# Unit 0's first loads, the clearing of padding and the table of steps in a kernel of gated linear attention followed by a rational feed-forward layer

## The chip, the cores and the metric

The kernel runs on one core of a Trainium2 chip. Its time is the device time of one execution in microseconds (us). The time before is the median of three runs; one further execution was taken with the hardware profiler, and its own time stands in the table below.

## What is computed

For each of 4 batches and 8 heads, with 768 time steps and 48 channels per head, a state of 48 x 48 is decayed and updated at each step, and read by q. The output of all heads, 3072 rows of 384, goes through two matrices with a rational function between them.

```python
f = 1.0 / (1.0 + np.exp(-f_logit))
for t in range(S):
    state = f[:, :, t, :, None] * state + np.einsum('bhd,bhe->bhde', k[:, :, t], v[:, :, t])
    y[:, :, t] = np.einsum('bhd,bhde->bhe', q[:, :, t], state)
...
h = x @ w_in                                   # 384 -> 2048
P = a[0] + a[1] * h + a[2] * h2 + a[3] * h3
Q = 1.0 + np.abs(b[0]) * np.abs(h) + np.abs(b[1]) * h2
out = (P / (Q + 1e-06)) @ w_out                # 2048 -> 384
```

## The kernel before

The work is cut into 12 units: 3 stretches of 256 time steps, each for the 4 batches in turn. Unit n + 4 continues the state of unit n. Within a unit, 256 steps are two chunks of 128 (index j), and the 8 heads are four pairs (index a).

Nothing is scheduled automatically. The string `ORDER` is a table of 815 steps, and the program is written out in that order. Each engine then works through its own instructions strictly in the order in which they stand, so the table alone sets what waits behind what. A step is a short name, the unit, and a range; `@0` to `@3` names one of four slots of PSUM, and a step that takes a slot waits until the slot's last reader is done.

The steps, with the engine that they run on, and the name of the tile by which the profile shows them:

- **Loads.** `ld n f`, `ld n k`, `ld n q` are issued on SP's DMA queue (L194), `ld n v` on POOL's, since it converts to bf16. `wi` and `wo` load the two weight matrices in pieces on POOL's queue (L201, four DMAs to a step, and L205). `ab_` loads the four numbers a and the two numbers b, copied to all 128 partitions, on SP (L209, L211).
- **Constants.** `ca`, `cb` build triangular masks and the identity on POOL. `cz` clears tiles on DVE with memsets (L232): `zeros`, `lsp`, `qkp`, `vmp` and the states. Of `lsp` and `qkp` each head has 64 columns, of which 48 are written later and 16 stay zero. `cc` builds a mask on DVE. `fa` and `fb` turn a and b into scaled coefficients `sig` on DVE, with one Ln on ACT (L264).
- **Attention, unit n.** `ef` and `ls`: Exp and Ln of the gates on ACT (L279 to fn, L284 to lsp). `cs`: sums over time on PE. `A n 0` and `A n 1`: Exp of these on ACT (L304, which needs `sig`, and L306). `xa n 0` and `xa n 1`: q and k times A, to qkp on DVE (L311). `T`, `Te`: transposes on PE (tp) and their copy on DVE (qkT, L330). `sc`, `mk`: scores on PE (L343) and their masking on DVE (scm, L351). `vm`: a shifted copy of v on POOL (vmp, L358). `ya`, `yb`: sv, the sums for the state, and y on PE; y needs qkT, scm and vmp. `ae`, `st`: the state's decay on ACT and the new state on DVE (L423). `ye`: y is copied to bf16 on ACT (xT, L414).
- **Feed-forward, unit n.** `h`: matmul with w_in on PE (hp, L432), 4 of 16 blocks to a step. `hy`: copy to bf16 on ACT (hy, L446). `sq` on DVE or `sa` on ACT: the square (h). `ab`: the absolute value on DVE (z, L458). The denominator z + h is summed on PE (`u`) and goes to `ln` on ACT (L474); or it is summed by `zd`, a DMA on POOL's queue that adds h into z (L483), or by `zv` on DVE, and goes to `lz` on ACT (lq, L490). `ex`: Exp on ACT (qi, L498). `p1`, `p2`, `pm`: the numerator's parts on DVE (gall and hy). `ta` adds them by a DMA on POOL's queue (L517), `tv` on DVE. `gm`: times qi on DVE (L526). `o`: matmul with w_out on PE (op, L533). `oe`: copy of the result (osb, L548), `so`: store on SP.

Unit 0 is loaded and worked on in two halves of the heads, `0 2` (the low ones) and `2 4` (the high ones).

Of the kernel before, what the change touches and what calls it, by code (L numbers as in the profile page):

```python
# [24 lines left out]
yb 0 2 4; st 0 1; yb 0 0 2; ld 2 q; ye 0; h 0 4 8 @2; ef 1; ld 2 f; ls 1; h 0 0 4 @3; hy 0 4 8
cs 1 @0; hy 0 0 4; h 0 8 12 @2; A 1 0; sq 0 0 8; A 1 1; p1 0 0 8; hy 0 8 12; h 0 12 16 @0; wo 4 8
xa 1 0; wo 12 16; ab 0 0 8; ld 2 k; wo 0 4; hy 0 12 16; xa 1 1; u 0 4 8 @2; wo 8 12; p2 0 0 8
T 1 @3; ln 0 4 8; p1 0 8 16; vm 1 0; ya 1 0 @0 @1; Te 1; ld 2 v; u 0 0 4 @2; ae 1; vm 1 1; ld 3 q
st 1 0; sc 1 0 @3; ln 0 0 4; ab 0 8 16; ya 1 1; mk 1 0; ld 3 f; ef 2; sc 1 1 @2; ex 0 0 8; mk 1 1
st 1 1; yb 1; sq 0 8 16; ls 2; ye 1; cs 2 @1; pm 0 0 8; u 0 12 16 @2; A 2 1; p2 0 8 16; u 0 8 12 @0  # L30
A 2 0; pm 0 8 16; ln 0 12 16; h 1 4 8 @3; ld 3 k; xa 2 0; ln 0 8 12; h 1 8 12 @2; tv 0 8 16
sa 1 4 8; h 1 12 16 @0; tv 0 0 8; hy 1 4 8; hy 1 8 12; xa 2 1; h 1 0 4 @1; hy 1 12 16; gm 0 0 8
T 2 @2; sa 1 0 4; ab 1 8 16; o 0 0 0 4 @0; sq 1 8 16; hy 1 0 4; o 0 0 4 8; ex 0 8 16; vm 2 0
o 0 1 0 4; Te 2; ld 3 v; u 1 8 12 @1; ab 1 0 8; vm 2 1; ld 4 q; u 1 12 16 @2; ln 1 8 12; p1 1 0 16
u 1 0 4 @3; ln 1 12 16; ld 4 f; gm 0 8 16; sc 2 1 @1; o 0 1 4 8; ef 3; pm 1 8 16; u 1 4 8 @2; ld 4 k
ln 1 0 4; o 0 1 8 12; mk 2 1; ls 3; o 0 0 8 12; ln 1 4 8; vm 3 1; o 0 0 12 16; p2 1 0 16; ld 4 v
cs 3 @1; ex 1 8 16; vm 3 0; o 0 1 12 16; ld 5 q; pm 1 0 8; ta 1 8 16; ya 2 0 @2 @3; ta 1 0 8; A 3 1
ld 5 f; ae 2; A 3 0; xa 3 1; ld 5 k; ef 4; st 2 0; sc 2 0 @1; xa 3 0; ya 2 1; oe 0 0 2 s; ls 4
mk 2 0; so 0 0 2; T 3 @0; ex 1 0 8; st 2 1; yb 2; Te 3; cs 4 @3; ld 6 q; vm 4 1; ye 2; ld 5 v
sc 3 0 @0; A 4 1; sc 3 1 @1; mk 3 0; vm 4 0; h 2 12 16 @2; A 4 0; mk 3 1; h 2 0 4 @3; hy 2 12 16  # L40
gm 1 8 16; ya 3 0 @1 @0; hy 2 0 4; xa 4 1; h 2 8 12 @2; sa 2 0 4; gm 1 0 8; ae 3; h 2 4 8 @3
hy 2 8 12; ld 6 f; st 3 0; xa 4 0; ef 5; ya 3 1; sa 2 4 8; ab 2 8 16; ld 6 k; T 4 @2; st 3 1; ls 5
sq 2 8 16; yb 3; hy 2 4 8; cs 5 @0; Te 4; ye 3; u 2 12 16 @3; ld 7 q; A 5 0; ab 2 0 8; h 3 12 16 @2
p1 2 0 16; ln 2 12 16; zd 2 0 8; sc 4 0 @1; ld 6 v; A 5 1; xa 5 0; h 3 0 4 @3; hy 3 12 16; vm 5 0
p2 2 0 16; ld 7 f; vm 5 1; u 2 8 12 @0; ef 6; hy 3 0 4; xa 5 1; h 3 4 8 @2; ld 7 k; pm 2 8 16
ln 2 8 12; o 1 0 0 4 @3; ld 8 q; hy 3 4 8; o 1 1 0 4; mk 4 0; ta 2 8 16; h 3 8 12 @0; ex 2 8 16
ab 3 0 8; pm 2 0 8; ya 4 0 @1 @2; hy 3 8 12; sq 3 0 8; ta 2 0 8; o 1 1 4 8; ls 6; sc 4 1 @0
ab 3 8 16; o 1 0 4 8; zd 3 0 8; ae 4; lz 2 0 8; mk 4 1; o 1 0 8 12; o 1 0 12 16; st 4 0; ld 8 f
cs 6 @0; ef 7; sq 3 8 16; ya 4 1; ex 2 0 8; p1 3 0 16; ld 8 k; yb 4; o 1 1 8 12; vm 6 0; st 4 1
ye 4; o 1 1 12 16; vm 6 1; pm 3 8 16; ld 7 v; u 3 8 12 @2; A 6 0; pm 3 0 8; oe 1 0 2 s; h 4 12 16 @1  # L50
ln 3 8 12; so 1 0 2; p2 3 0 16; u 3 12 16 @3; hy 4 12 16; h 4 8 12 @2; xa 6 0; ta 3 8 16; ln 3 12 16
gm 2 8 16; ld 9 q; h 4 0 4 @1; A 6 1; ta 3 0 8; hy 4 8 12; gm 2 0 8; T 5 @0; sa 4 0 4; xa 6 1
o 2 0 0 4 @2; hy 4 0 4; Te 5; o 2 0 4 8; lz 3 0 8; o 2 1 0 4; sq 4 8 16; sc 5 1 @0; o 2 1 4 8
ld 9 f; mk 5 1; o 2 1 8 12; ef 8; ya 5 0 @1 @3; ex 3 0 8; ld 9 k; ab 4 8 16; zv 4 8 16; sc 5 0 @0
# [12 lines left out]
hy 6 0 4; mk 7 1; o 4 1 8 12; ex 5 0 8; zv 6 8 16; o 4 1 12 16; ya 7 0 @3 @0; ab 6 0 8; sa 6 0 4
p1 6 0 16; o 4 0 4 8; ae 7; o 4 0 8 12; ls 9; zd 6 0 8; st 7 0; o 4 0 12 16; ex 5 8 16; p2 6 0 16
ya 7 1; yb 7; pm 6 8 16; oe 4 0 2 s; cs 8 @1; vm 9 0; ye 7; st 7 1; cs 9 @2; so 4 0 2; vm 9 1
pm 6 0 8; ld 10 v; A 8 1; h 7 4 8 @3; A 8 0; xa 8 1; ta 6 8 16; h 7 0 4 @0; ef 11; xa 8 0; ta 6 0 8  # L70
ld 11 k; hy 7 4 8; h 7 12 16 @1; gm 5 8 16; ld 11 q; hy 7 0 4; gm 5 0 8; A 9 0; T 8 @3; hy 7 12 16
h 7 8 12 @0; xa 9 0; A 9 1; Te 8; o 5 0 0 4 @1; lz 6 0 8; o 5 1 0 4; sq 7 0 8; sc 8 0 @3; sc 8 1 @2
mk 8 0; hy 7 8 12; o 5 1 4 8; o 5 1 8 12; ex 6 0 8; mk 8 1; o 5 0 4 8; ya 8 0 @3 @0; ab 7 8 16
lz 6 8 16; xa 9 1; o 5 0 8 12; p1 7 0 16; o 5 0 12 16; o 5 1 12 16; ae 8; ls 10; st 8 0; T 9 @2
# [40 lines left out]
def kernel(  # L115
# [113 lines left out]
    def zero(t):  # L229
        f = t.rearrange({2: "p a -> p a", 3: "p a b -> p (a b)", 4: "p a b c -> p (a b c)",  # L230
                         5: "p a b c d -> p (a b c d)"}[len(t.shape)])
        nc.vector.memset(f.bitcast(F32), 0.0)  # L232

    def const_z(i):
        if i == 0:
            zero(zeros)
            zero(lsp[0])
            nc.vector.memset(ind, 0.0)
# [349 lines left out]
```

## Time and profile before

| what | value |
| --- | --- |
| median of 3 runs | 240.35 us (240.1 to 240.41) |
| the profiled execution's own time | 242.23 us |
| its span, from the first to the last instruction | 240.5 us |
| mean granted TensorE clock | 0.984 |
| DMA moved, mean rate | 41.61 MB, 173 GB/s |

The page of the profile gives busy times by engine over the span, the chain of work that ended last, and groups of like instructions. A wait is put down to the instruction or the DMA that released it last. Tile names are those of the list above, with buffer numbers left out; `x4` is a count.

### The profile page before, as it was taken

The numbers are of one execution on the slowest core, as the hardware profiler recorded it, in microseconds if no ns is written. First come the engines' busy times: TensorE is split into PE (matmuls) and PEld (weight loads), VectorE is DVE, ScalarE is ACT, GpSimd is POOL, SyncE is SP. The second block draws the span as 40 slices with busy tenths as digits, with TensorE's granted clock in tenths as the row PEclk, the third lists the DMA queues.
The fourth block names the chain that finished last, engine by engine and source line by source line (L and its number), as shares of the span: only waits on it lengthen the run. The fifth ranks groups of instructions, "written<-read, shape, count | busy, mean of one in ns | idle before, by whom it ended". The sixth has DMA issues, their size and how long they took to land.

```text
span 240.5 us, 7105 instructions
## 1 busy us (share of the span) xinstructions
PE 213.5 (89%) x3107; PEld 148.8 (62%) x3120; DVE 205.7 (86%) x241; ACT 206.3 (86%) x214; POOL 79.4 (33%) x101
## 2 busy tenths in 40 slices
PE   0188997999899999999998999999999799999981
PEld 0065664855687766768657668667676576665540
DVE  7473299998889999989999899999999799989730
ACT  3323668999889999999999999999996999989870
POOL 8657300845120732202149525032151104322200
PEclk9999997999799999999999999999999999999999
DMA  7999999994999999999399999938929254989854
GB/s 134 221 227 230 200 204 204 224 198 34 201 208 213 173 257 216 228 231 166 59 164 200 257 198 183 238 96 107 191 69 175 47 112 92 192 159 192 182 113 121
DMA packets 62430, 41.61 MB, mean 173 GB/s; under 512 B 51520, under 2 KB 58176, under 8 KB 62400
## 3 DMA queue, kind: packets, MB, share of 16 engines
q0 software_dynamic: 21136, 22.29, 57.4%
q1 hardware_dynamic: 41264, 18.88, 32.9%
q8 instruction: 24, 0.39, 0.7%
q14 instruction: 6, 0.05, 0.1%
HBM read 25.17 MB, written 4.72 MB: 124 GB/s over the span
## 4 chain that ended last, share of the span: by engine, by line
ACT 29%; DVE 26%; PE 26%; issue 8%; DMA 8%; SPq 1%; ACTq 0%; DVEq 0%
PE hp L432 9%; ACT hy L446 7%; DMA z<-h 6%; ACT qi L498 6%; PE op L533 5%; ACT lq L474 5%; DVE qkp L311 4%; ACT lq L490 4%; DVE scm L351 4%; ACT h L454 3%; DVE gall L526 3%; PE y L364 3%; DVE z L458 2%; DMA b_sb<-in_moe_b_dram 2%; PE tp L322 2%
## 5 line engine op out<-in xcount | busy, mean ns | idle before, releaser
L432 PE MATMUL hp<-xT,w_in_sb 128*128 128x256 bf16 x576 | 70.3, 279 | 2.4 <-issue 1.1
L533 PE MATMUL op<-w_out_sb,gall 128*128 128x384 bf16 x384 | 68.8, 327 | 2.3 <-ACT lq L474 0.7
L432 PEld LDWEIGHTS <-w_in_sb 128*128 128x128 bf16 x576 | 56.6, 100 | 13.8 <-issue 3.3
L446 ACT CAST hy<-hp 128x1024 bf16<-128x1024 f32 x48 | 48.5, 1050 | 4.6 <-PE hp L432 4.4
L533 PEld LDWEIGHTS <-gall 128*128 128x128 bf16 x384 | 35.7, 98 | 26.5 <-issue 2.2
L498 ACT ACTIVATE qi<-lq 128x2048 bf16<-128x2048 f32 (+1 forms) x25 | 46.4, 1872 | 0.1
L358 POOL COPY vmp<-vn 128x128 bf16<-128x128 bf16 x24 | 24.0, 1015 | 68.1 <-PE y L364 29.0
L526 DVE TENSOR_TENSOR gall<-gall,qi 128x2048 bf16<-128x2048 bf16 (+1 forms) x25 | 29.2, 1176 | 5.3 <-ACT qi L498 4.2
L517 POOL DMA_DIRECT2D gall<-hy x23 | 20.5, 969 | 38.5 <-DVE gall L513 16.5
L351 DVE TENSOR_TENSOR scm<-sc,mask 128x1024 bf16<-128x1024 f32 x24 | 28.8, 1217 | 1.7 <-PE sc L343 1.6
L490 ACT ACTIVATE lq<-z,sig 128x2048 f32<-128x2048 bf16 x13 | 26.5, 2039 | 3.5 <-DMA z<-h 3.5
L513 DVE TENSOR_TENSOR gall<-gall,h 128x2048 bf16<-128x2048 bf16 (+1 forms) x25 | 29.2, 1176 | 0.0
L450 DVE TENSOR_TENSOR h<-hy 128x2048 bf16<-128x2048 bf16 (+1 forms) x17 | 19.8, 1164 | 8.1 <-ACT hy L446 8.1
L474 ACT ACTIVATE lq<-u,sig 128x1024 f32<-128x1024 f32 x22 | 24.7, 1138 | 0.8 <-PE u L466 0.7
L483 POOL DMA_DIRECT2D z<-h x10 | 11.2, 1119 | 35.8 <-DVE z L458 28.7
L294 PE MATMUL cs<-lsp,Ui 128*128 128x384 bf16 (+1 forms) x39 | 11.2, 353 | 11.4 <-ACT lsp L284 11.4
L503 DVE TENSOR_SCALAR gall<-hy,a_sb 128x4096 bf16<-128x4096 bf16 (+2 forms) x15 | 16.9, 1127 | 0.3 <-ACT hy L446 0.3
L458 DVE TENSOR_SCALAR z<-hy 128x2048 uint16<-128x2048 uint16 (+1 forms) x25 | 16.5, 665 | 0.6 <-ACT hy L446 0.3
L454 ACT ACTIVATE h<-hp 128x1024 bf16<-128x1024 f32 x16 | 17.0, 1060 | 0.0
L508 DVE TENSOR_SCALAR hy<-hy,a_sb 128x4096 bf16<-128x4096 bf16 (+2 forms) x15 | 16.8, 1126 | 0.0
L330 DVE COPY qkT<-tp 128x2048 bf16<-128x2048 bf16 (+1 forms) x13 | 14.8, 1136 | 2.3 <-PE tp L322 2.3
L322 PE MATMUL tp<-ident,qkp 128*128 128x128 bf16 x192 | 14.6, 235 | 0.1
(70 smaller groups left out, 288.6 us busy)
## 6 DMA issues: line engine op xcount, KB each, us to landing
gall<-hy POOLq DMA_DIRECT2D x21, 512.0 KB, 6.8
z<-h POOLq DMA_DIRECT2D x10, 512.0 KB, 6.3
qn<-in_q_dram SPq DMA_DIRECT2D x11, 384.0 KB, 10.2
fn<-in_f_logit_dram SPq DMA_DIRECT2D x11, 384.0 KB, 8.9
kn<-in_k_dram SPq DMA_DIRECT2D x11, 384.0 KB, 10.2
out_dram<-osb SPq DMA_DIRECT2D x22, 192.0 KB, 2.9
vn<-in_v_dram POOLq DMA_DIRECT2D x12, 192.0 KB, 6.9
w_in_sb<-in_moe_w_in_dram POOLq DMA_DIRECT2D x16, 96.0 KB, 6.7
```

The source lines that it names most:

```text
L351: nc.vector.tensor_mul(t, s["sc", g].rearrange("s r a i t -> s (r a) (i t)"), mb)
L358: nc.gpsimd.tensor_copy(s["vm"][:, :, :, 32 * x:32 * x + 16], src)
L432: nc.tensor.matmul(t[:, m - m0, :].rearrange("f (j t) -> f j t", j=UB), w_in_sb[:, kk, m * P:(m + 1) * P], s["x"][:, :, kk, :], start=(kk ...
L446: nc.scalar.copy(fl(big(s, "hy", "hy", 3), m0, m1), fl(s["hp", m0], 0, m1 - m0))
L454: nc.scalar.activation(fl(big(s, "h2", "h2", 2), m0, m1), fl(s["hp", m0], 0, m1 - m0), AF.Square)
L458: nc.vector.tensor_scalar(fl(big(s, "z", "z", 2), m0, m1).bitcast(U16), fl(s["hy"], m0, m1).bitcast(U16), 0x7FFF, None, op0=ALU.bitwise_and)
L474: nc.scalar.activation(fl(s["lq", g], m0 - 8 * g, m1 - 8 * g), fl(s["u", m0], 0, m1 - m0), AF.Ln, scale=sig[:, 2:3], bias=1.0 + 1e-6)
L490: nc.scalar.activation(fl(s["lq", g], m0 - 8 * g, m1 - 8 * g), fl(s["z"], m0, m1), AF.Ln, scale=sig[:, 2:3], bias=1.0 + 1e-6)
L498: nc.scalar.activation(fl(s["qi", g], m0 - 8 * g, m1 - 8 * g), fl(s["lq", g], m0 - 8 * g, m1 - 8 * g), AF.Exp, scale=-1.0)
L513: nc.vector.tensor_mul(fl(s["g"], m0, m1), fl(s["g"], m0, m1), fl(s["h2"], m0, m1))
L526: nc.vector.tensor_mul(fl(s["g"], m0, m1), fl(s["g"], m0, m1), fl(s["qi", g], m0 - 8 * g, m1 - 8 * g))
L533: nc.tensor.matmul(s["op"][:, j, 0:DM], s["g"][:, m, C * j:C * j + C], w_out_sb[:, m, :], start=(m == 0), stop=(m == KF - 1))
```

## The change

Three things are changed.

The padding: `cz` clears only the 16 padding columns of each head of `lsp` and `qkp`, and of `vmp` the 16 columns in the middle. The tile `zeros` and the step `warm`, which the table did not use, are gone.

The first loads: `ab_` now stands ahead of all loads on SP. The queue there was q 2 4, f 2 4, q 0 2, k 2 4, b, a, f 0 2, k 0 2, and is now b, a, k 0 2, f 2 4, f 0 2, q 0 2, k 2 4, q 2 4. On POOL the triangular masks and the identity now come ahead of the first load of v; then come twelve loads of w_in, v of unit 1, the first `vm` of unit 0, the last four loads of w_in, and the second `vm`. Before, both `vm` of unit 0 stood behind the first four loads of w_in.

The table: the same 815 steps with the same ranges, in another order and with other slots. The order came from a model of the kernel in which DMAs of the two issuing queues, SP's and POOL's, now take turns.

```diff
 ORDER = """
-cz 2; cb; ld 0 q 2 4; ld 0 v; ld 0 f 2 4; ld 0 q 0 2; ca; ld 0 k 2 4; cz 3; cz 1; ab_; ld 0 f 0 2
...
+cz 0; ca; ab_; ld 0 k 0 2; cz 2; ld 0 f 2 4; ld 0 f 0 2; cz 1; cb; cz 3; ld 0 q 0 2; ld 0 v; fa
...
-    zeros = consts.tile([P, 512], BF16, name="zeros")
...
     def const_z(i):
+
+        if i == 3:
+            for t in states:
+                zero(t)
+            return
+        for x in ((0,), (0,), (1,))[i]:
+            if i != 1:
+                nc.vector.memset(lsp[x][:, :, :, D:64].bitcast(F32), 0.0)
+            if i != 0:
+                nc.vector.memset(qkp[x].rearrange("p x i h d -> p (x i h) d")[:, :, D:64].bitcast(F32), 0.0)
+                nc.vector.memset(vmp[x][:, :, :, 16:32].bitcast(F32), 0.0)
         if i == 0:
-            zero(zeros)
-            zero(lsp[0])
             nc.vector.memset(ind, 0.0)
...
-        elif i == 1:
-            zero(qkp[0])
-            zero(vmp[0])
-        elif i == 2:
-            zero(lsp[1])
-            zero(qkp[1])
-            zero(vmp[1])
...
```

Three places where the new table moves instructions.

The first is DVE in unit 0, from a qkp (q or k times A, one half of the heads) to the last new state. Before:

```order
L311 TENSOR_TENSOR qkp_88<-qn,A_186 128x2x4x48
L330 COPY qkT<-tp 128x4x256
L311 TENSOR_TENSOR qkp_88<-qn,A_186 128x2x4x48
L311 TENSOR_TENSOR qkp_88<-kn,A_180 128x2x4x48
L351 TENSOR_TENSOR scm_240<-sc,mask 128x1024
L330 COPY qkT<-tp 128x4x256
L423 TENSOR_TENSOR state_94<-sv,alast 128x384
L351 TENSOR_TENSOR scm_301<-sc,mask 128x1024
L423 TENSOR_TENSOR state_94<-sv,alast 128x384
```

And now, where A_177 belongs to q and A_188 to k:

```order
L304 TENSOR_TENSOR qkp_87<-qn,A_177 128x2x4x48
L304 TENSOR_TENSOR qkp_87<-kn,A_188 128x2x4x48 x2
L323 COPY qkT<-tp 128x4x256
L416 TENSOR_TENSOR state_93<-sv,alast 128x384
L344 TENSOR_TENSOR scm_261<-sc,mask 128x1024
L304 TENSOR_TENSOR qkp_87<-qn,A_177 128x2x4x48
L323 COPY qkT<-tp 128x4x256
L344 TENSOR_TENSOR scm_328<-sc,mask 128x1024
L416 TENSOR_TENSOR state_93<-sv,alast 128x384
```

Before, all four products stood ahead of the first masking of scores; now the last one, q of the high heads, stands behind the low heads' masking.

The second is ACT from the xT of unit 2 on. Before (A belongs to unit 4, hy and h to unit 2):

```order
L414 CAST xT<-y 128x768
L306 ACTIVATE A_1134<-cs 128x768
L304 ACTIVATE A_1169<-cs,sig 128x768
L446 CAST hy<-hp 128x1024 x2
L454 ACTIVATE h_1231<-hp 128x1024
```

And now, where qi and lq belong to unit 1:

```order
L407 CAST xT<-y 128x768
L491 ACTIVATE qi<-lq 128x2048
L467 ACTIVATE lq<-u,sig 128x1024
L447 ACTIVATE h_1138<-hp 128x1024
L439 CAST hy<-hp 128x1024 x2
```

The two A of unit 4 now stand ahead of xT, and feed-forward work of unit 1 lies between xT and the first use of hp.

The third is ACT late in the program, from the lq of unit 9 that reads z to the one of unit 10. The DMA that adds h into unit 10's z is issued after the first of them has begun. Before:

```order
L490 ACTIVATE lq<-z,sig 128x2048
L414 CAST xT<-y 128x768
L498 ACTIVATE qi<-lq 128x2048
L474 ACTIVATE lq<-u,sig 128x1024
L446 CAST hy<-hp 128x1024 x2
L490 ACTIVATE lq<-z,sig 128x2048
```

And now:

```order
L483 ACTIVATE lq<-z,sig 128x2048
L439 CAST hy<-hp 128x1024
L491 ACTIVATE qi<-lq 128x2048
L407 CAST xT<-y 128x768
L483 ACTIVATE lq<-z,sig 128x2048
```

One lq and one hy fewer lie between the two readers of z.

More of the change, by code (lines that the diff above doesn't have):

```diff
@@ L25 @@
[L25 to L30, printed above, removed]
```

173 lines of the change are left out of this document (86 added, 87 removed).

## Prediction

> **What bounds the kernel now.** I read the page first: the busy shares and the chain that ended last.
>
> ```profile
> span 240.5 us, 7105 instructions
> PE 213.5 (89%) x3107; PEld 148.8 (62%) x3120; DVE 205.7 (86%) x241; ACT 206.3 (86%) x214; POOL 79.4 (33%) x101
> ACT 29%; DVE 26%; PE 26%; issue 8%; DMA 8%; SPq 1%; ACTq 0%; DVEq 0%
> ```
>
> Three engines share the chain almost evenly, so no single one can be relieved with much effect. The stages tell more; columns are the stretch, then busy time of PE, PEld, DVE, ACT and POOL, the granted clock, the DMA share and GB/s.
>
> ```profile
> 64.00:66.00 2.00, 2.00 (x75) 1.57 (x73) 1.33 (x2) 1.26 (x2) 0.23 (x1) 0.65 0.99 196
> 68.00:70.00 2.00, 2.00 (x33) 1.61 (x31) 2.00 (x3) 1.34 (x3) 0.00 (x0) 1.00 1.04 249
> 160.00:180.00 20.00, 19.92 (x298) 13.94 (x283) 20.00 (x21) 20.00 (x22) 7.94 (x9) 1.00 0.70 130
> 180.00:200.00 20.00, 18.64 (x295) 13.13 (x296) 17.60 (x19) 17.88 (x17) 2.49 (x3) 1.00 0.50 101
> ```
>
> From 160 to 180 us ACT and DVE have no idle time at all. What the table of steps can win lies in the start, in stretches such as 64 to 70, and where ACT waits for a DMA. I asked who ACT waited for between 28 and 100 us (two rows), and between 100 and 224 us (the third); columns are the total, the times, the longest.
>
> ```profile
> ACT hy L446 <- PE hp L432: 3.0, 5, 1.5
> ACT xT L414 <- PE y L364: 1.0, 2, 0.7
> ACT lq L490 <- DMA z<-h: 3.5, 3, 2.1
> ```
>
> So in 196 us ACT waits 7.5 us by these rows alone, and the largest late part is for the accumulating DMA z<-h. Then the start, from the timeline (start, duration):
>
> ```profile
> 2.95 0.52 SPq L209 DMA_DIRECT2D b_sb<-in_moe_b_dram  x1
> 3.52 0.43 SPq L211 DMA_DIRECT2D a_sb<-in_moe_a_dram  x1
> 4.35 0.52 ACT L279 ACTIVATE fn<-fn 128x384 f32<-128x384 f32 x1 [2.26 <-DMA fn<-in_f_logit_dram]
> 6.25 0.52 ACT L284 ACTIVATE lsp<-fn 128x384 bf16<-128x384 f32 x1 [1.38 <-DVE ind L238]
> 8.91 0.22 DVE L255 TENSOR_SCALAR bm<-b_sb 128x2 uint32<-128x2 uint32 x1 [2.51 <-DMA b_sb<-in_moe_b_dram]
> 10.36 0.47 ACT L306 ACTIVATE A<-cs 128x384 f32<-128x384 f32 x1
> 11.15 0.57 ACT L304 ACTIVATE A<-cs,sig 128x384 f32<-128x384 f32 x1
> 14.94 0.55 DVE L311 TENSOR_TENSOR qkp<-kn,A 128x384 bf16<-128x384 f32 x1
> 15.19 1.03 PE L322 MATMUL tp<-ident,qkp 128*128 128x128 bf16 x8
> 16.32 2.24 POOL L201 DMA_DIRECT2D w_in_sb<-in_moe_w_in_dram  x4 [2.56 <-DMA w_in_sb<-in_moe_w_in_dram]
> 16.54 0.68 DVE L330 COPY qkT<-tp 128x1024 bf16<-128x1024 bf16 x1
> 17.33 0.64 PE L343 MATMUL sc<-qkT 48*64 48x128 bf16 x16
> 18.12 1.22 DVE L351 TENSOR_TENSOR scm<-sc,mask 128x1024 bf16<-128x1024 f32 x1
> 21.19 0.80 ACT L414 CAST xT<-y 128x768 bf16<-128x768 f32 x1 [3.58 <-PE y L364]
> ```
>
> The forget gates are ready early (Exp at 4.35), but the coefficient chain starts only at 8.91, when b_sb lands, and ACT's queue stands behind it until 10.36. This is the wait that the change goes for. The first finished block of unit 0 is xT at 21.19.
>
> **The change part by part.**
>
> Coefficients first. The loads of b and a now stand ahead of everything on SP. They take the queue from 2.95 to 3.99, so 1.04 us, and the gate load f 2 4, which stands two places later than before (b, a, k instead of q), is issued 1.04 us later; its Exp moves from 4.35 to 5.4. When b lands is not shown for an empty queue; these rows bound it (KB, us to landing):
>
> ```profile
> b_sb<-in_moe_b_dram SPq DMA_DIRECT2D x1, 1.0 KB, 5.9
> out_dram<-osb SPq DMA_DIRECT2D x4, 96.0 KB, 2.2
> ```
>
> Issued at 0.82, b lands between 3.0 and 6.7; nothing is queued ahead of it, so I take the lower end. The vector chain and the Ln need 10.36 - 8.91 = 1.45 us, so the coefficients stand at 4.5, at worst at 8.2. The first A needs two Exp and two Ln of 0.52 on ACT from 5.4 on: 7.5. So the coefficients are off the path unless b takes over 5.2 us. The Trainium skill, page "DMA: Bandwidth & Descriptors", section "Specifications", says that a transfer under 512 B runs below line rate, which speaks against 256 rows of 8 and 16 B at the head of the queue; no row here prices it, and the b row of 5.9 us had four loads ahead of it.
>
> From 7.5 on I follow the new DVE order (the first of the changed places shown above). Two A (0.57 and 0.47), then the third of 0.57 until 9.1; qkp for q and k of the low heads, 0.5 each, 10.1. In the old run the transposes were done 0.73 after the last qkp (14.94 + 0.55 to 16.22): 10.85. Before sc there come sv and its companions, 1.1 in the old run (16.22 to 17.33): 11.95, sc until 12.6, scm until 13.8. Only then qkp of q's high heads, 14.3, transposes 15.05, copy 15.75, sc 16.4, scm 17.65. In the old run xT started 1.85 after the last scm (18.12 + 1.22 to 21.19): 19.5, a gain of 1.7 us. The old order had the two halves side by side, the new one has them in line, which is why 2.9 us at the first A shrink to 1.7.
>
> A new cover: both vmp copies, which y needs, now stand on POOL behind weight loads, the second behind all sixteen and the load of the next v. The row at 16.32 shows what this costs: POOL had issued eight DMAs that had not landed, and waited 2.56 us for one. With the same limit the second copy comes at about 19 (an estimate: the ninth to eighteenth issue each wait for the landing of the one eight places ahead, and these land no closer than they were issued, 2.24 / 4 = 0.56 us apart). Then some 1.1 of the 1.85 us between scm and xT is left, and xT stands at 20.3: gain 0.9. Between 0.9 and 1.7 I take **-1.3**; the ends are -2.0 and, with k or v late, +0.5.
>
> Padding only. A memset that shrinks is worth this:
>
> ```profile
> L232 DVE MEMSET qkp<- 128x1024 f32 x2 | 1.8, 912 | 0.3 <-issue 0.3
> L232 DVE MEMSET lsp<- 128x512 f32 x2 | 1.0, 485 | 1.0 <-PEq L572 1.0
> ```
>
> The slope is (912 - 485) / 512 = 0.83 ns a column, so qkp falls to 256 columns, 0.27 us each, lsp to 128, 0.17: about 2.4 us less on DVE with zeros gone. All of it lies in the first 6 us, where DVE then waits for b. I cost it at **0**: without it the coefficients would stand at most 2.4 us later than 4.5, at 6.9, still ahead of the A at 7.5.
>
> The table. First, unit 2: in the old order ACT goes from xT to A to hy and waits there; the two stretches quoted show 0.74 and 0.66 us idle at a granted clock of 0.65 in the first. In the new order qi and lq stand behind xT, so the matmuls have 3 us to run. This is worth up to 1.4.
>
> Second, the accumulates. ACT's cover between the issue of z<-h and its use is counted from the order, with means of these rows (x count, busy, mean ns):
>
> ```profile
> L446 ACT CAST hy<-hp 128x1024 bf16<-128x1024 f32 x48 | 48.5, 1050 | 4.6 <-PE hp L432 4.4
> L498 ACT ACTIVATE qi<-lq 128x2048 bf16<-128x2048 f32 x23 | 44.4, 1942 | 0.1
> L474 ACT ACTIVATE lq<-u,sig 128x1024 f32<-128x1024 f32 x22 | 24.7, 1138 | 0.8 <-PE u L466 0.7
> L414 ACT CAST xT<-y 128x768 bf16<-128x768 f32 x12 | 9.9, 824 | 4.6 <-PE y L364 4.6
> L264 ACT ACTIVATE sig<-sig 128x1 f32<-128x1 f32 x1 | 0.2, 203 | 3.5 <-DVE sig L261 3.5
> ```
>
> The twenty ACT groups, from 48.5 down to 0.2, add to 230 us where ACT is busy 206.3: neighbours overlap, factor 0.9. For unit 10 (third place above) the cover was xT, qi, lq and two hy, 0.9 x 6.0 = 5.4; now it is hy, qi and xT, 0.9 x 3.8 = 3.4. Done so for units 2 to 11, the old covers are 9.0, 13.4, 7.0, 8.9, 10.1, 5.4, 4.5, 6.6, 5.3, 6.2, the new ones 4.1, 7.0, 5.3, 9.2, 4.6, 4.6, 9.5, 5.9, 3.4, 4.3. Against them stands:
>
> ```profile
> z<-h POOLq DMA_DIRECT2D x10, 512.0 KB, 6.3
> z<-h POOLq DMA_DIRECT2D x1, 512.0 KB, 4.5
> z<-h POOLq DMA_DIRECT2D x1, 512.0 KB, 10.2
> ```
>
> the median, the shortest, and one behind two others on its queue. With 6.3 the old covers fall short by 3.8 in all (measured: 3.5), the new ones by 11.9: 8.1 more. With 4.5 it is 1.7 more. I take the middle, +4.9. But while ACT waits for a landing, PE and DVE run on, and the waits of ACT for them (the 4.0 of the two rows above, unit 2's among them) become shorter. I take all 4.0 off: net **+0.9**, ends -2.5 and +5.
>
> Third, the end. In the old order the copy of unit 9's output stands between lq and the last qi of unit 11; now it is ahead of the last z, inside its wait.
>
> ```profile
> 229.57 0.80 ACT L548 COPY osb<-op 128x768 f32<-128x768 f32 x1
> ```
>
> Of 0.80 I take **-0.6**, ends 0 and -0.8.
>
> Sum: -1.3 + 0 + 0.9 - 0.6 = -1.0. The profiled execution took 242.23 us, of which 1.7 lie around the span; it would take 241.2. It is 1.9 above the median of the runs, 240.35, and the gain carries over: **239.4 us**.
>
> **The rivals.**
>
> The landings fit the new covers. These rows bear on it, the first for the accumulate issued at 77.9 us beside loads, the second for the loads of q as a group.
>
> ```profile
> z<-h POOLq DMA_DIRECT2D x1, 512.0 KB, 5.8
> qn<-in_q_dram SPq DMA_DIRECT2D x11, 384.0 KB, 10.2
> ```
>
> An accumulate beside loads is not as slow as the loads are. If most land near the shortest, 4.5, then 1.7 is added, 4.0 goes, and -1.3 and -0.6 stay: 236.2. The Trainium skill, page "DMA: Bandwidth & Descriptors", section "Queues, rings and completion order", says that each DMA engine takes turns between the queues it has work for, so an accumulate need not wait behind the loads of SP; the trace agrees, with 5.8 beside loads of 10.2, and by that rule this case would hold.
> Against it stand the other 10.2, that of an accumulate behind two others of its own queue, and the median of 6.3. Chance 0.18.
>
> The accumulates come late. At ten places ACT, which is full from 160 on, stands in order before lq<-z; each microsecond by which the landing exceeds the cover is added, and qi, gall and the output matmuls behind it are late with it. With 6.3 everywhere and only 4.0 taken off: 240.35 - 1.3 + 8.1 - 4.0 - 0.6 = 242.6. It decides for slower once the average landing passes some 5.7 us. For it speaks that the old covers predict the old waits within 0.3 us; against it that ACT's instruction then running adds up to 2 us of cover. Chance 0.34.
>
> The start wins nothing. If the second vmp copy comes after 20 us, behind weights that POOL cannot issue, xT is no earlier than 21.2 and the sum is +0.3: 240.7. Chance 0.12. The coefficient wait is then gone and nothing is won.
>
> **How the numbers follow.** The forecast, 238 to 240.2, has 0.36. A measurement of this kernel cannot tell differences under about 0.2%, 0.5 us. Faster: most of the forecast, 0.32, and all of the first rival, 0.18: 0.50. Same: 0.04 and most of the third, 0.10: 0.14. Slower: 0.34 and 0.02: 0.36. For 8 in 10 the range goes from the first rival's 236.2 a little down, 235.9, to 243.6, the second's 242.6 with the start's upper end in part.
>
> **What would show it.** Right: bm<-b_sb starts at 3 to 4 us, the first A at 7 to 8, xT at 19.5 to 20.5; ACT's waits for z<-h grow beyond 3.5 in all while those for hp and y fall. Wrong: the first A still behind sig; xT at 21 or later with POOL waiting for w_in ahead of vmp; z<-h waits over 9 us in all (slower), or under 3.5 (faster than forecast); new waits of DVE for gall<-hy or of PE for w_out, which now comes later on POOL, that I cost at nothing.

## The result, and the profile after

| kernel | median (range) | ratio to before, 95% interval |
| --- | --- | --- |
| before | 240.22 us (239.04 to 240.41) | |
| after | 248.56 us (247.18 to 250.96) | 1.0339 [1.0257, 1.0421] |

The change makes the kernel 3.4% slower. Some executions of every kernel are over 1.5% longer than its fastest: the medians in the tables are of all executions and the ratios of the others alone (so that new_rest further down has 250.22 us beside 1.0295), and the profile of before, 242.23 us, is of a longer execution than the profile of pad_only, 239.21 us, which has the same table of steps. The profiled execution of after took 247.18 us, the fastest of its four runs, with a span of 245.5. Its page, the lines that answer to those of before:

```profile
span 245.5 us, 7102 instructions
PE 213.0 (87%) x3104; PEld 146.3 (60%) x3120; DVE 205.7 (84%) x240; ACT 206.9 (84%) x214; POOL 74.1 (30%) x101
DVE 23%; ACT 22%; DMA 21%; PE 19%; issue 13%; POOL 1%; SPq 1%; ACTq 0%; DVEq 0%
DMA z<-h 10%; DMA gall<-hy 9%; PE hp L425 6%; ACT hy L439 6%; ACT qi L491 5%; PE op L526 5%; DVE qkp L304 3%; DVE gall L519 3%; DVE gall L506 3%; DVE scm L344 3%; PE y L357 2%; DVE z L451 2%; ACT lq L483 2%; DVE state L416 2%; DVE gall L496 2%
```

PE, DVE and ACT do the same work for as long as before (213.5, 205.7 and 206.3 us there). Everything that is lost is idle time. On the chain that ended last, DMA went from 8% to 21%, and nearly all of it is the two accumulating DMAs. What ACT waited for in after, and DVE below it, between 28 us and the end (total, times, longest):

```profile
ACT lq L483 <- DMA z<-h: 9.7, 7, 3.4
DVE gall L519 <- DMA gall<-hy: 7.1, 5, 3.4
```

In before ACT's row was 3.5, and DVE's, between 28 us and 224, this:

```profile
DVE gall L526 <- DMA gall<-hy: 1.1, 2, 0.7
```

So ACT waits 6.2 us more for z, and DVE 6.0 more for gall. Against the profile of pad_only, where the two rows are 1.9 and 2.8, it is 7.8 and 4.3: some 12 us together either way, but how they split changes with the execution. The stretches of after show where (busy PE, PEld, DVE, ACT, POOL, clock, DMA share, GB/s):

```profile
60.00:80.00 20.00, 17.00 (x271) 12.53 (x271) 16.02 (x17) 15.37 (x17) 8.28 (x9) 1.00 1.16 239
160.00:180.00 20.00, 18.75 (x290) 12.65 (x288) 18.94 (x20) 18.20 (x20) 6.85 (x7) 1.00 0.82 146
180.00:200.00 20.00, 19.81 (x389) 14.80 (x382) 20.00 (x21) 20.00 (x20) 3.49 (x4) 1.00 0.45 97
```

and the first of them in before:

```profile
60.00:80.00 20.00, 18.64 (x389) 14.66 (x390) 18.31 (x21) 18.47 (x24) 4.26 (x7) 0.91 1.02 209
```

From 60 to 80 us ACT lost 3.1 us against before (18.47 to 15.37), and from 160 to 180, where it had been full, 1.8. From 180 to 200 it is the other way (20.00, where before had 17.88), since the same work now stands later. The timeline of after shows what happens between 60 and 84 (all waits of DVE, PE and ACT above 1 us there; the last column is the wait ahead of the instruction), and below it the median time to landing of the two accumulates of unit 1, issued at 62.3 and 63.2 (8.1 us for the first, so 10.2 for the second):

```profile
70.54 1.23 DVE L519 TENSOR_TENSOR gall<-gall,qi 128x2048 bf16<-128x2048 bf16 x1 [3.41 <-DMA gall<-hy]
72.29 0.35 PE L357 MATMUL y<-qkT,state 128*32 128x128 bf16 x12 [2.64 <-DVE state L416]
74.73 0.90 ACT L297 ACTIVATE A<-cs,sig 128x768 f32<-128x768 f32 x1 [1.66 <-PE cs L287]
80.42 2.01 ACT L483 ACTIVATE lq<-z,sig 128x2048 f32<-128x2048 bf16 x1 [3.40 <-DMA z<-h]
```

```profile
gall<-hy POOLq DMA_DIRECT2D x2, 512.0 KB, 9.2
```

One landing stops all three engines in turn. DVE stands at gall (3.41) with the next unit's work queued behind; PE then waits for the state that DVE had not made (2.64), ACT for the sums that PE had not made (1.66). DVE's absolute value of unit 2 comes late too (72.15), so its z<-h goes out only at 73.4, and ACT meets it too early (3.40).

The start of after, from its timeline:

```profile
3.40 0.17 DVE L253 TENSOR_SCALAR bm<-b_sb 128x2 uint32<-128x2 uint32 x1 [0.34 <-DMA b_sb<-in_moe_b_dram]
5.00 0.20 ACT L262 ACTIVATE sig<-sig 128x1 f32<-128x1 f32 x1 [2.92 <-DVE sig L259]
7.82 0.58 ACT L297 ACTIVATE A<-cs,sig 128x384 f32<-128x384 f32 x1
14.12 0.55 DVE L304 TENSOR_TENSOR qkp<-qn,A 128x384 bf16<-128x384 f32 x1
17.58 0.30 POOL L351 COPY vmp<-vn 128x128 bf16<-128x128 bf16 x1
20.06 0.80 ACT L407 CAST xT<-y 128x768 bf16<-128x768 f32 x1 [7.57 <-PE y L357]
```

It is as foretold, 1.1 us earlier than before. But in the six other profiles with the same first steps (gm_later, new_start, small_new and three more below) xT stands at 21.8 to 22.7, later than the 21.19 of before; this execution is the exception. And 21.19 is not fixed either: pad_only, with the old table, has its xT at 20.50.

### The profile page after: what moved, and what is told of

Same layout as the page of the kernel before. It is cut to its first block, busy times and chain, and to the rows that moved or that the text cites. A ratio compares the mean times of both kernels' runs of the same rounds, so it can differ in the third digit from the quotient of the medians.

```text
span 245.5 us, 7102 instructions
## 1 busy us (share of the span) xinstructions
PE 213.0 (87%) x3104; PEld 146.3 (60%) x3120; DVE 205.7 (84%) x240; ACT 206.9 (84%) x214; POOL 74.1 (30%) x101
## 4 chain that ended last, share of the span: by engine, by line
DVE 23%; ACT 22%; DMA 21%; PE 19%; issue 13%; POOL 1%; SPq 1%; ACTq 0%; DVEq 0%
DMA z<-h 10%; DMA gall<-hy 9%; PE hp L425 6%; ACT hy L439 6%; ACT qi L491 5%; PE op L526 5%; DVE qkp L304 3%; DVE gall L519 3%; DVE gall L506 3%; DVE scm L344 3%; PE y L357 2%; DVE z L451 2%; ACT lq L483 2%; DVE state L416 2%; DVE gall L496 2%
## 5 line engine op out<-in xcount | busy, mean ns | idle before, releaser
L510 POOL DMA_DIRECT2D gall<-hy x23 | 21.2, 1071 | 64.0 <-DVE hy L501 23.1
L519 DVE TENSOR_TENSOR gall<-gall,qi 128x2048 bf16<-128x2048 bf16 (+1 forms) x25 | 29.8, 1192 | 11.8 <-DMA gall<-hy 7.1
L351 POOL COPY vmp<-vn 128x128 bf16<-128x128 bf16 x24 | 18.9, 819 | 33.6 <-issue 13.4
L476 POOL DMA_DIRECT2D z<-h x10 | 9.4, 944 | 39.1 <-ACT h L447 9.2
L451 DVE TENSOR_SCALAR z<-hy 128x2048 uint16<-128x2048 uint16 (+1 forms) x25 | 17.0, 686 | 2.8 <-ACT hy L439 2.8
L193 POOL DMA_DIRECT2D vn<-in_v_dram x12 | 12.8, 1067 | 18.4 <-issue 18.2
L315 PE MATMUL tp<-ident,qkp 128*128 128x128 bf16 x192 | 13.7, 226 | 3.9 <-DVE qkp L304 3.2
```

What stands on the lines that cost most here:

```text
L451: nc.vector.tensor_scalar(fl(big(s, "z", "z", 2), m0, m1).bitcast(U16), fl(s["hy"], m0, m1).bitcast(U16), 0x7FFF, None, op0=ALU.bitwise_and)
L510: nc.gpsimd.dma_start(out=fl(s["g"], m0, m1), in_=fl(s["hy"], m0, m1), accum_op=ALU.add)
L519: nc.vector.tensor_mul(fl(s["g"], m0, m1), fl(s["g"], m0, m1), fl(s["qi", g], m0 - 8 * g, m1 - 8 * g))
```

## The experiments

The theories that the expectations name: theory 1, ACT and DVE read the accumulates before they have landed; theory 2, the loss comes from somewhere else, told in each; theory 3, the tiny rows of the coefficients hold up the first loads; theory 4, early weight loads do.

| kernel | median | ratio to before, 95% interval |
| --- | --- | --- |
| pad_only | 240.32 | 0.9992 [0.9954, 1.0029] |
| new_start | 244.23 | 1.0175 [1.0114, 1.0237] |
| new_rest | 250.22 | 1.0295 [1.0208, 1.0383] |
| gm_later | 249.82 | 1.0421 [1.0366, 1.0476] |
| small_old | 238.19 | 0.9925 [0.9890, 0.9959] |
| small_new | 239.21 | 1.0001 [0.9971, 1.0032] |
| z_small_new | 246.25 | 1.0199 [1.0134, 1.0263] |
| small_new_1to3 | 243.38 | 1.0154 [1.0113, 1.0195] |
| old_lz_early | 257.02 | 1.0681 [1.0626, 1.0737] |
| lz_early_small | 245.90 | 1.0265 [1.0216, 1.0314] |
| lz_later | 252.94 | 1.0524 [1.0475, 1.0573] |
| coef_first | 242.29 | 1.0088 [1.0045, 1.0131] |
| new_start_ab_late | 244.03 | 1.0141 [1.0082, 1.0200] |
| new_start_vm | 240.59 | 1.0024 [0.9991, 1.0057] |
| new_start_ab_act | 240.46 | 1.0026 [0.9992, 1.0060] |
| old_ab_act | 242.27 | 1.0107 [1.0053, 1.0162] |
| after_start_fixed | 252.55 | 1.0523 [1.0466, 1.0579] |
| old_ab_row | 238.80 | 0.9952 [0.9919, 0.9986] |

### One part of the change alone

pad_only has the new clearing with the old table.

> The changed clearing of padding alone, with the whole old table. Prediction's costing at nothing: 240.2, within 0.5 of the kernel before. If clearing narrow strided columns costs DVE or delays the first steps: over 241. The wait for b_sb stays as it was.

It is no different from before (the interval reaches 0.5% down and 0.3% up): the padding was costed rightly.

new_start has the new table up to the last step of unit 0's attention (`ye 0`) and the old order behind it; new_rest the other way round.

```diff
-cz 2; cb; ld 0 q 2 4; ... ; ye 0; <old rest>
+cz 0; ca; ab_; ld 0 k 0 2; ... ; ye 0; <old rest>     new_start
+cz 2; cb; ld 0 q 2 4; ... ; ye 0; <new rest>          new_rest
```

> The changed kernel with the new table up to the first xT (unit 0), and from there on the old table's steps in the old order. Theory 1 (the loss lies in the table after unit 0, where accumulating DMAs land later than their cover): xT comes at about 20.1 us instead of 21.2 and the rest runs as before, so 239.1, about 1.1 under the kernel before, with waits of ACT for z<-h near the old 3.5. Theory 2 (the loss is sown in the start: weights and v later on POOL, loads in another order): 245 or more.

> The changed kernel with the old table up to the first xT, and from there on the new table's steps. Theory 1: the whole loss is here and the start's gain of 1.1 is missing, so 249 to 250, with waits of ACT for z<-h near 9.7 and of DVE for gall<-hy near 7. Theory 2: near 241.

The start, in which I had seen the whole gain, costs 1.75%, and the rest of the table 2.95%; the two intervals overlap, so which is more is not settled. new_start came out near theory 2's number, new_rest nearer to theory 1's (247.3 us by the ratio). ACT's waits for z in new_rest are 11.2 us, but DVE's for gall only 2.5, where near 7 were expected. The two costs do not add up simply, since a join of two tables is a third order.

### Short accumulates

In four kernels one or both accumulates move one of eight row blocks, 64 KB in place of 512. Steps and order stay.

```diff
-        nc.gpsimd.dma_start(out=fl(s["z"], m0, m1), in_=fl(s["h2"], m0, m1), accum_op=ALU.add)
+        nc.gpsimd.dma_start(out=fl(s["z"], m0, m0 + 1), in_=fl(s["h2"], m0, m0 + 1), accum_op=ALU.add)
...
-        nc.gpsimd.dma_start(out=fl(s["g"], m0, m1), in_=fl(s["hy"], m0, m1), accum_op=ALU.add)
+        nc.gpsimd.dma_start(out=fl(s["g"], m0, m0 + 1), in_=fl(s["hy"], m0, m0 + 1), accum_op=ALU.add)
```

> Leaves out seven eighths of both accumulations by DMA (512 KB becomes 64 KB: only the first of each eight row blocks is added), in the kernel before; all instructions and their order stay. In before, ScalarE waits 3.5 us for z and VectorE 1.1 us for g. Theory 1 (in after the landings come later than the new table's covers allow; in before they fit): little is won here, 237.5 to 240 us, ratio 0.99 to 1.0 of before. Theory 2 (the loss of after is in the order of TensorE's work, landings do not matter): same numbers here; the pair with small_new decides.

> The same cut of both accumulations in the changed kernel, whose waits for z are 9.7 us (ScalarE) and for g about 7.3 us (VectorE). Theory 1: these waits go and nearly all of the loss behind unit 0 with them; only the cost of the new start stays (new_start was 3.7 us over before): 0 to 4 us over small_old, about 239 to 243 us. Theory 2 (order of TensorE's work): other waits take their place and it stays 6 us or more over small_old, 244 us or more.

With short accumulates the two tables are 1.0 us apart (238.19 and 239.21; by the two ratios 1.8) where they were 8.3 apart. The waits of small_new, ACT's and DVE's, and its accumulates (KB, us to landing):

```profile
ACT lq L484 <- DMA z<-h: 3.7, 2, 2.0
DVE gall L520 <- DMA gall<-hy: 1.3, 1, 1.3
gall<-hy POOLq DMA_DIRECT2D x23, 64.0 KB, 2.6
z<-h POOLq DMA_DIRECT2D x10, 64.0 KB, 2.4
```

So most of the loss hangs on the accumulates, and theory 2's order of TensorE's work is out as its main cause. The cut takes their traffic away as well as their length, which this pair does not separate. ACT's row for z is still 3.7 here, where small_old has none, and yet the two are 1.0 to 1.8 us apart: the sum of one engine's waits is not the price by itself.

The other two ask which accumulate, and where.

> The changed kernel with only the accumulate into z cut to one of eight row blocks (64 KB), the one into g as it is; leaves out seven eighths of the sum of the denominator. after is 8.3 us over before, small_new (both cut) 0. If both kinds count by the waits that they end (ScalarE 9.7 us for z, VectorE 7.1 for g): 242 to 245 us. If z alone makes the loss: 239 to 241.5. If g alone: 246 to 249.

> The changed kernel with short accumulates (64 KB) for units 1, 2 and 3 alone, the others as they are; leaves out seven eighths of those units' accumulation. In the profiles of after and small_new, which have the same order, xT falls back by some 3 us between units 2 and 4, 2 us at units 6 and 7, and some 3 us behind unit 11. Theory 1 with each wait added where it arises: 3 to 4 us faster than after, 244.5 to 245.5 us. Rival (a delay won early is lost again at the next short cover, the late ones decide): 247 to 249 us.

With z alone cut, the ratio falls from 1.034 to 1.020, 3.4 us of some 8 (and to 245.0 us by the ratio, at the upper end of what was expected if both kinds count). Its own waits, and how long its short z and its long gall took:

```profile
ACT lq L484 <- DMA z<-h: 3.2, 3, 1.6
DVE gall L520 <- DMA gall<-hy: 8.9, 8, 2.9
gall<-hy POOLq DMA_DIRECT2D x21, 512.0 KB, 6.8
z<-h POOLq DMA_DIRECT2D x10, 64.0 KB, 4.4
```

Cutting gall as well, as small_new does, takes the other 4.8 (1.020 to 1.000). So about half of the loss, or more, hangs on what DVE waits for, which the prediction left out. The intervals are too wide to say which half is larger, and gall was not cut alone. A z of 64 KB still takes 4.4 us when gall's 512 KB stand on the same queue, against 2.4 when both are short. That the place on the queue does it, and not the traffic, is not shown. With the accumulates of units 1 to 3 alone cut, the ratio is 1.015, so 4.4 us of some 8 are gone, a little more than the 3 to 4 expected: about half of the loss hangs on the accumulates of these three units, the cascade at 70 us above among them, and it is not caught up later.

### The reading step moved

```diff
-ta 1 8 16; ... ; gm 1 0 8; ... ; sq 2 8 16
+ta 1 8 16; ... ; sq 2 8 16; gm 1 0 8                   gm_later, in after
-zd n 0 8; ... ; lz n 0 8; ...
+zd n 0 8; ... ; ... ; lz n 0 8                         lz_later, seven units in after
+zd n 0 8; lz n 0 8; ... ; ...                          old_lz_early, eight units in before
```

> The changed kernel with one step moved: the product gall<-gall,qi of unit 1's low half goes behind the two new states and the square of unit 2 in DVE's queue, so that DVE need not stand 3.4 us for the landing of gall<-hy at 67 us. Theory 1 with a cascade (that wait holds up the states, PE's y, ACT's A and the issue of unit 2's z): the waits of 3.4 on DVE, 2.6 on PE, 1.7 and 3.4 on ACT between 67 and 80 us largely go, and the time falls by 2 to 3.5 us against the changed kernel's 248.6. Rival (the waits only move to the next landing): it falls by less than 0.7 us.

> The changed kernel with only that Ln moved later, for units 2, 4, 6, 7, 9 and 10, up to the Exp that reads it: covers of 4.9, 6.1, 7.0, 5.5, 6.8, 6.9 us instead of 4.1, 5.3, 4.6, 4.6, 5.9, 3.4. Theory 1: the shortfall against 6.3 us falls from 11.9 to about 4 us; 2 to 6 us faster than after's 248.6, so 243 to 246.5 us. Rival (as when one gm was moved: the wait moves on to the next reader, VectorE's qi and g): 247.5 to 250 us.

> The kernel before with one kind of step moved: the Ln that reads z (lz n 0 8) stands earlier for units 2, 3, 4, 6, 7, 9, 10 and 11, so that ScalarE's cover between the issue of the accumulate and this read is as short as in after or shorter (4.4, 7.0, 5.1, 4.9, 3.6, 5.7, 3.5, 4.5 us). Nothing else moves. Theory 1 (short covers make the loss): with landings of 6.3 us the shortfall grows by some 10 us; ScalarE's waits for z come over 9 us and the kernel to 244 to 249 us. Rival (the waits for z only take the place of other waits, and the loss of after comes from VectorE's waits for g or from TensorE's order): 240 to 242 us.

> old_lz_early (the old table with the Ln on z of eight units earlier; 257.0 us, 16.8 over before) with both accumulations cut to one of eight row blocks, 64 KB instead of 512; leaves out seven eighths of the accumulation. Theory 1 (the landings make the loss): 238 to 241 us, as small_old with 238.2. Rival (the earlier Ln itself takes ScalarE from the copies and Exp that TensorE and VectorE wait for): 246 us or more.

Neither of the two repairs in after worked. In gm_later the cascade at 70 us went as intended: DVE's 3.41, PE's 2.64 and ACT's 1.66 are gone, which bears out that one landing made all three, and DVE's waits for gall fell from 7.1 to 3.0 us in all. But the kernel is as slow as after or slower, and ACT's waits for z rose from 9.7 to 12.3, the longest now at unit 3 (3.56, where after had 0.19): the wait moved on. In the row of gm_later's page, the numbers behind the second bar are the idle time ahead of these instructions and the part of it that ended with z<-h:

```profile
L484 ACT ACTIVATE lq<-z,sig 128x2048 f32<-128x2048 bf16 x13 | 26.3, 2021 | 12.3 <-DMA z<-h 12.3
```

lz_later moves the Ln of seven units, the six named and unit 11. It is 4 us slower than after, outside both expectations, though ACT's waits for z fell to less than half, near the 4 us counted beforehand; in its profile, from 28 us on:

```profile
ACT hy L440 <- PE hp L426: 5.3, 4, 1.5
ACT lq L484 <- DMA z<-h: 4.5, 3, 3.3
ACT xT L408 <- PE y L358: 2.9, 2, 1.6
```

9.7 us of waits for z became 4.5, and 8.2 us of waits for PE came in their place. A later Ln makes the Exp, gall and the output matmuls later, and those stand ahead of hp and y on PE; that this is the way is argued, not shown.

The reverse goes the way that theory 1 says, and further than either expectation. With the Ln earlier in the old table the kernel is 16.8 us slower, twice as much as after. lz_early_small, the same order with both accumulates short, tells how that splits: 257.0 to 245.9, so 11.1 us go with the accumulates (10.0 by the ratios), of which 2.0 go in the old table as well (small_old). That is near the shortfall of some 10 us counted beforehand, but ACT's waits for z came to 6.0 only, not to the 9 expected, so most of it shows up in other waits. And 245.9 is 7.7 us above small_old, the rival's number and not theory 1's: this is the price of an ACT instruction of 2.0 us standing ahead of other work at eight places. I had put that at nothing in the expectation for old_lz_early. ACT's rows in old_lz_early and, in the second fence, in lz_early_small:

```profile
ACT xT L415 <- PE y L365: 6.2, 3, 4.4
ACT lq L491 <- DMA z<-h: 6.0, 5, 3.3
```

```profile
ACT xT L415 <- PE y L365: 3.6, 4, 1.5
ACT lq L491 <- DMA z<-h: 0.2, 1, 0.2
```

### The start

> The kernel before with one step moved: the two small loads of the coefficients stand first in the table. Theory 3 (256 rows of 8 and 16 bytes at the head of SyncE's queue hold up every load behind them by 1 to 2 us, and the first stage is bound by those loads): 0.5 to 3 us slower than before, 241 to 243.5 us, first data rate of 150 GB/s and more one to two us later than in before. The prediction's reason (the rows cost nothing, the first A comes earlier): 0.5 to 1.5 us faster, 239 to 240 us.

coef_first moves nothing but `ab_` to the head of the old table. It is 2.1 us slower: theory 3's sign and size. Its own rates from 2 to 5 us are 1, 32 and 120 GB/s, and those of before 205, 296 and 132. The rates at the start (the last number is GB/s), in pad_only, whose SP queue begins with q, f, q, k, in new_start, whose queue begins with b and a, and in new_start_ab_act, where b and a stand on ACT's queue:

```profile
2.00:3.00 1.00, 0.00 (x0) 0.00 (x0) 0.59 (x4) 0.09 (x1) 0.93 (x3) 1.00 0.85 207
3.00:4.00 1.00, 0.00 (x0) 0.10 (x1) 0.36 (x2) 0.00 (x0) 0.86 (x4) 1.00 1.07 268
4.00:5.00 1.00, 0.00 (x0) 0.00 (x0) 0.51 (x4) 0.62 (x2) 0.93 (x4) 1.00 1.25 157
```

```profile
2.00:3.00 1.00, 0.00 (x0) 0.00 (x0) 1.00 (x6) 0.09 (x1) 0.86 (x4) 1.00 0.05 1
3.00:4.00 1.00, 0.00 (x0) 0.00 (x0) 0.65 (x3) 0.00 (x0) 1.00 (x2) 1.00 0.31 48
4.00:5.00 1.00, 0.00 (x0) 0.00 (x0) 0.86 (x7) 0.01 (x1) 1.00 (x3) 1.00 0.91 213
```

```profile
2.00:3.00 1.00, 0.00 (x0) 0.00 (x0) 1.00 (x6) 0.09 (x1) 0.86 (x4) 1.00 0.59 110
3.00:4.00 1.00, 0.00 (x0) 0.00 (x0) 0.06 (x1) 0.00 (x0) 1.00 (x2) 1.00 0.61 143
4.00:5.00 1.00, 0.00 (x0) 0.00 (x0) 0.54 (x4) 0.00 (x0) 1.00 (x3) 1.00 0.42 105
```

With 256 rows of 8 and 16 bytes ahead, 262 KB move from 2 to 5 us (1 + 48 + 213) in place of 632 (207 + 268 + 157). From ACT's queue it is 358: the loads now move beside the rows from 2 us on (110 GB/s in place of 1), so the rows no longer stand wholly in front.

The Trainium skill, page "DMA: Bandwidth & Descriptors", section "Specifications", has transfers under 512 B below line rate, and the section "Rules for kernel authors" says that spreading DMAs over issuing engines wins no bandwidth since all use the same DMA engines. The first agrees with these rows in its direction, but it does not set the tiny rows apart: in pad_only all 1834 packets from 2 to 5 us are under 512 B too, and they move the 632 KB. The second agrees in part: from ACT's queue 358 KB move, more than 262 and far fewer than 632.

> new_start (new table up to ye 0, then the old one; 244.2 us, 3.7 over before) with the loads of the coefficients moved behind the first three loads of SyncE's queue, so that k and f of unit 0 go first. Theory 3: most of the 3.7 us goes, 240 to 242 us, xT of unit 0 before 21.5 us in the profile. Rival (the order of the k, f and q loads and of unit 0's steps costs the 3.7 us): 243.5 to 245 us, xT of unit 0 at 22 us or later.

> new_start (new table up to ye 0, old one behind it; 244.2 us) with the two vm of unit 0 behind the first four loads of w_in on POOL's queue, as the old table has them, so that three of the seven weight loads that went out at 4 to 8 us come later. Theory 4 (these weight loads take the DMA engines from k and q of unit 0, which then land at 12.8 and 15.2 us instead of 8 to 11): k by 11 us, xT of unit 0 before 21.3 us, 241 to 242.5 us. Rival (the weights have no part in it): no change, 243.5 to 245 us, xT at 22 us or later.

> new_start with the two small loads of the coefficients issued from ScalarE's own DMA queue instead of SyncE's, at the same place; nothing else moves. Theory 3 (their 256 tiny rows hold up the queue that they stand in): the first data rate over 150 GB/s comes before 3.5 us instead of after 4, k, f and q land 1 to 2 us earlier, xT before 21.5 us, 241.5 to 243 us. Rival (the rows hold up the DMA engines, not the queue, or the rest of the new start costs the time): 243.5 to 245 us, landings as in new_start.

```diff
-cz 0; ca; ab_; ld 0 k 0 2; cz 2; ld 0 f 2 4; ld 0 f 0 2; cz 1; cb
+cz 0; ca; ld 0 k 0 2; cz 2; ld 0 f 2 4; ld 0 f 0 2; ab_; cz 1; cb     new_start_ab_late
...
-ld 0 k 2 4; wi 8 12; ef 0 2 4
+ld 0 k 2 4; wi 8 12; vm 0 0; vm 0 1; ef 0 2 4                         new_start_vm
...
-        nc.sync.dma_start(out=b_sb, ...
+        nc.scalar.dma_start(out=b_sb, ...                             new_start_ab_act, a_sb too
```

new_start_ab_late won nothing, and does not decide between its two expectations: with b behind three loads, b landed at 6.8 us, and in the new table ACT's Ln of `fa` stands ahead of the first Exp, so sig came at 8.13 and all of ACT behind it. One delay took the place of another. The other two each took the start's loss away (240.59 and 240.46): so in the new start the loss needs both the tiny rows at the head of SP's queue and the early weight loads, of which theories 3 and 4 name one each. In new_start this is what waited, and when xT came:

```profile
12.81 0.56 DVE L306 TENSOR_TENSOR qkp<-kn,A 128x384 bf16<-128x384 f32 x1 [1.81 <-DMA kn<-in_k_dram]
22.25 0.80 ACT L409 CAST xT<-y 128x768 bf16<-128x768 f32 x1 [7.57 <-PE y L359]
```

k of the high heads landed at 12.8 us, behind the tiny rows and beside seven weight loads that POOL sent out from 4.1 to 8.0. With vm ahead of three of those it landed at 12.3 and q at 13.1 in place of 15.2; with the rows on ACT's queue k at 9.1 and q at 12.1. xT came at 21.86 and 21.08. In new_start_vm 0.4 us of unit 0's xT were worth 3.6 us of the whole, so that xT alone does not carry the start's cost: the load of k for unit 1 landed at 16.4 in place of 21.3, and unit 2's xT came at 65.62 in place of 67.77.

> The kernel before with the coefficients first and on ScalarE's DMA queue, nothing else moved (coef_first, which has them first on SyncE's queue, was 2.1 us slower than before). Theory 3 (tiny rows hold up the queue that they stand in, not the others): loads as in before, the first A at 7 to 8 us instead of 10.4, xT of unit 0 at 19.5 to 20.5, 238.5 to 240 us. Rival (unit 0 is bound by the loads of k and q, not by the coefficients): within 0.5 us of before, xT at 21 us or later.

> The changed kernel with the two edits that each took the start's 3.7 us off new_start: the coefficients on ScalarE's DMA queue, and both vm of unit 0 behind the first four weight loads. If the start's delay adds to the later waits: 244.5 to 246.5 us. Rival (the delay of the start lies beneath the waits for landings and is not added): 247.5 to 249.5 us.

Neither held. old_ab_act is 2.7 us slower than before in its own rounds (239.61), 1.1% by the ratio, no better than coef_first: the Exp of f of the high heads starts at 7.06 us (4.35 in pad_only), that of the low ones at 12.66 (10.04). So the rows cost what they cost from either queue, and theory 3 as I had written it, by the queue, is wrong. What ACT's queue won in new_start it probably won because k stood first on SP there, but no run shows this. after_start_fixed is 252.55, slower than after, outside both expectations. PE's wait between 20 and 46 us:

```profile
PE hp L426 <- DMA w_in_sb<-in_moe_w_in_dram: 3.1, 1, 3.1
```

With vm forward POOL sends eight loads of w_in only from 11.9 us on, and PE's wait ends at 23.95, when one that was issued at 15.8 has landed 8.0 us later; new_start_vm, with xT a microsecond later, has no such wait. A repair that fits one order can be a fault in the other; that this wait makes up the 4 us against after is not shown.

The last one loads the coefficients as two rows, spreads them by a matmul with ones, and puts their chain ahead of the first sums, in the old table with the new clearing.

```diff
+        nc.sync.dma_start(out=ab_row[:, 0:2], in_=bass.AP(tensor=moe_b.tensor, offset=moe_b.offset,
+                                                          ap=[[0, 1]] + list(moe_b.ap)))
...
+        t = slot(3, [P, 6], F32, "abp")
+        nc.tensor.matmul(t, ones, ab_row, start=True, stop=True)
+        nc.vector.tensor_copy(b_sb, t[:, 0:2])
+        nc.vector.tensor_copy(a_sb, t[:, 2:6])
```

> The old table with the new clearing, the coefficients loaded first but as one row of two and one of four numbers, spread to the 128 partitions by a matmul with ones, and their chain (fa) put ahead of the first sums. If the 256 rows are what costs (coef_first 2.1 us slower, old_ab_act 2.7): loads land as in before (f at 4.3, k at 7.9), the first A at 8 to 9 us instead of 10.4, xT at 20 to 20.8, 238.8 to 240 us. Rival (any load ahead of the others costs as much, or unit 0 is bound by k and q anyway): 240.2 us or more, xT at 21 us or later.

```profile
5.44 0.17 DVE L265 TENSOR_SCALAR bm<-b_sb 128x2 uint32<-128x2 uint32 x1
7.06 0.49 ACT L311 ACTIVATE A<-cs 128x384 f32<-128x384 f32 x1
19.85 0.80 ACT L419 CAST xT<-y 128x768 bf16<-128x768 f32 x1 [3.58 <-PE y L369]
```

The first A stands at 7.06 (10.36 in before), xT at 19.85 (21.19), and 238.80 us is 0.5% under before, the interval just clear of 1. Of these kernels that compute the whole it is the only one faster than before: what the change meant to win at the start is there, 1.2 us by the ratio and 1.4 by the medians, with rows that are two and not 256. Against pad_only, whose first A and xT stand at 9.66 and 20.50, the xT is 0.65 us earlier. The rows and the place of `fa` were changed together; which of them wins it was not separated.

## Why the prediction was wrong

**The step that failed first** is the offset: "I take all 4.0 off", for ACT's waits for PE that would vanish beneath its waits for landings. The rows named there did vanish, but these came between 28 and 100 us:

```profile
ACT lq L467 <- PE u L459: 2.7, 2, 1.8
ACT A L297 <- PE cs L287: 1.9, 2, 1.7
```

ACT's waits for other things in that stretch were 5.9 us in before (hy, xT, lq, alast, A) and 5.3 in after (these two and 0.7). So 0.6 went, not 4.0. In pad_only, with the old table, these waits are 3.7 us in the same stretch, 2.4 of them for hy and xT; against that execution nothing went, and the 4.0 was in part a matter of the execution. The premise that PE and DVE run on while ACT waits failed with it: in after PE waits 3.5 us for the state from DVE and 2.0 for hy from ACT, so after a few instructions each engine needs what another would have done.

**The second** is the wait of DVE for gall<-hy, named at the end of the prediction as costed at nothing. It went from 1.1 to 7.1 us (from 2.8 by pad_only), and by z_small_new beside small_new the accumulate into gall is worth 4.8 of some 8 us. The covers were counted for z alone, on ACT alone, though gall's accumulates are 23 against 10 and share the queue.

**The gross term** was counted soundly and sized too low. The covers with a landing of 6.3 gave 8.1 us more of waits for z; measured were 6.2. The middle of 4.9 rested on landings near 4.5, which after does not show (for z 5.1 at the shortest and 6.4 in the median, and 8.1 and 10.2 for the two of unit 1's gall). So the waits were foretold fairly (7.8 more against pad_only). What they cost the kernel is another matter: in small_new and lz_later ACT's waits for z and the time do not go together.

**The start**: the steps up to the first A came as foretold, b at 3.40, sig at 5.00, A at 7.82 (8.3 to 8.8 in the six other profiles), and vmp at 17.58 was not in the way. Wrong was to price b and a by their issue alone, 1.04 us, and to leave k and q out of the path but for an end of +0.5. By new_start the start costs +3.7 us by itself (4.2 by the ratio), not -1.3. The Trainium skill's 512 B sentence, quoted beside that step, spoke the right way, though by that threshold alone the loads behind the rows would be slow as well.

**Right** were the padding (0), unit 2's waits (its xT came at 59.64 in place of 65.77), and the end: from the last Ln on z to the end of the span it is 16.1 us (229.42 to 245.5) in place of 16.8 (223.73 to 240.5), 0.7 where 0.6 stood.

**The rivals**: "the accumulates come late" named the mechanism and the sign. Its 242.6 was 6 us low by the same two steps: it took the 4.0 off and left gall out. "The landings fit" fell with the landings: the rule of turns that it drew on speaks of different queues, and the two of unit 1 that took 8.1 and 10.2 us stood on one, beside loads, in a stretch of 239 GB/s.

**Open** stays whether it is the accumulates' length or their traffic; why gm_later won nothing once the cascade at 70 us was gone, beyond that the wait moved on; how much of new_start's 3.7 us is still in after, where the joint kernel's own waits lie over it; and why lz_later lost 4 us.

## What to carry to other kernels

Do not take it that a wait which one engine gets in a tightly interleaved program is paid for by waits of the others: price it in full, and then follow it once round the ring of engines, since at 70 us one landing idled three of them. Nor is a repair of one wait a gain: in gm_later and lz_later the waits went and the time did not, so only a run of the whole table tells. Count the cover of every asynchronous transfer, for each engine that reads one, against the landing time behind its neighbours on the queue. To move a small broadcast load to the front, make it few rows first; a price by bytes or by issue time misses it.

## What the runs showed of the hardware

Two loads of 256 tiny rows (3 KB together) cut what moved from 2 to 5 us from 632 KB to 262, and did so in part from another queue; as two rows they cost less: 39, 259 and 186 GB/s in old_ab_row. How much varied with the execution of the same steps: 14, 142 and 303 GB/s in the three microseconds in after's, 1, 48 and 213 in new_start's, and the xT that go with them stand at 20.06 and 22.25. An accumulate of 64 KB landed after 2.4 us with short neighbours on its queue and after 4.4 with long ones.
